# One small copy of the gates' weights, six times on GpSimd instead of ScalarE

## The chip, the cores and the metric

The kernel is one program on one core of a Trainium2 chip. A core has five engines, each with its own stream of instructions: TensorE (PE in the profile; its weight loads are PEld), VectorE (DVE), ScalarE (ACT), GpSimd (POOL) and SyncE (SP), which here only issues transfers. An engine executes its stream strictly in order; an instruction that waits for another engine or a transfer (a DMA) holds back all that stand behind it on its own engine. The metric is the device time of one launch in microseconds.

## The reference

For each of 8 batches `x` (2496 rows of 256 features, float32) is filtered in the frequency domain, and the result goes through a mixture of 8 experts, of which each row uses the two with the highest gate:

```python
X = np.fft.rfft(x, axis=1)
y = np.fft.irfft(X * (filt_r + 1j * filt_i)[None], n=x.shape[1], axis=1)

x = y.reshape(B * S, D)
noisy = x @ w_gate + np.log1p(np.exp(x @ w_noise)) * noise
top2 = np.argpartition(-noisy, 2, axis=1)[:, :2]      # softmax over these two: top2_w
for e in range(E):
    for k in range(2):
        mask = top2[:, k] == e
        h = np.maximum(x[mask] @ w1[e], 0.0)
        out[mask] += top2_w[mask, k, None] * (h @ w2[e])
```

Result: 19968 rows of 256 float32.

## The kernel before, in words

**The filter.** The transforms of a batch are matrix products with constant tables (2496 = 39 x 64). Features are taken in two halves of 128; `n` counts halves of batches, so `n` = 0 and 1 are batch 0, and `n % 2` (`h`) says which half. For each half the steps are: `s1` (L339, and L388 for its evictions), `kg1` (L417, with the filter applied by VectorE in L435 and L436), `kg2` (L457; the eviction into `G` is L459), then `t3` and `i2`. `t3` (L541) transposes `G` on TensorE into a PSUM tile, and ScalarE copies that to the tile `tf` (L546). `i2` (L563) multiplies by the last table, and ScalarE copies the product into the tile `yt` (L575). From `yt` SyncE writes up to 4 x 117 rows of the result to the array `y` in memory (L582). `t3` and `i2` run six times in a half, for 22 groups of rows (five times four groups, once two).

**The gates.** For the second half of a batch `yt` has 8 columns more, and into these goes `dense`, the weight that each expert has for the row; a row of `y` so carries what the experts need later. That is L580, a copy of 117x32 numbers (117x16 the last time), which stands between L575 and L582. `dense` comes from the gating of the batch: logits (L469, L479, L510), an exponential on ScalarE (L824, which first loads an activation table), and a chain of small VectorE operations that ends in L845. In parallel VectorE computes ranks (L835), and TensorE counts with them (L848 to L850) where each row goes in the lists of its experts. `slots` (L931, L932, L958) and `route` (L1000 to L1026; TensorE in L981 and L1017) turn this into the lists of rows, which GpSimd writes to memory with an indirect transfer (L1029, `lst`).

**The tiles.** In `n` = 0 the `yt` tiles lie in three places of other tiles that are not yet in use; for odd `n` they share two buffers (L572, `bufs=2`). So the third `yt` of a second half can be written only when the first has been read by its transfer, and so on.

**The experts.** A list is read back (L1050, `lt`), made into row numbers (L1058), and four indirect gathers fetch 128 rows each from `y` (L1096). GpSimd reorders halves of numbers (L1148) and takes the weights (L1115, `gt`). TensorE transposes the rows (L1156, `xps`), ScalarE and VectorE split them into a high part `mxh` (L1159) and a low part, and then come the two matrix products with each expert's weights: `hps` and `yps` (L126 to L128 in both, L1282 and L1283 for `yps` later on). Expert blocks start while the filter still works on later batches, and the two are interleaved.

**The order.** What stands where on an engine is fixed when the program is built. For the first batches a plan (`fft_stream`, with `at(slot, ...)`) lists the steps by slot and `pin` holds their instructions on each engine in the order in which they were written; the gating and the routing are placed freely between them. A timeline that the builder keeps for all engines decides where such free instructions go, and a different engine for one instruction changes this timeline for what follows. L580 is one of the instructions that `pin` holds in order on its engine.

Of the kernel before, what the change touches and what calls it, by code (L numbers as in the profile page):

```python
# [148 lines left out]
class Moe:  # L149
# [405 lines left out]
    def i2(self, n, g0):  # L555
        nc, P, h = self.nc, self.P, n % 2
        Dh, Dl = self.cD
        th, tl = self.t3t.pop((n, g0))
        k = min(4, NG - g0)
        m = 128 * k  # L560
        p = self.ps("q6")
        if tl is None:
            nc.tensor.matmul(p[:RP, :m], self.rD, th[:120, :m], start=True, stop=True)  # L563
        else:
            nc.tensor.matmul(p[:RP, :m], Dh, th[:120, :m], start=True, stop=False)  # L565
            nc.tensor.matmul(p[:RP, :m], Dh, tl[:120, :m], start=False, stop=False)  # L566
            nc.tensor.matmul(p[:RP, :m], Dl, th[:120, :m], start=False, stop=True)  # L567
        w = 128 + E * h
        if n == 0:
            yt = P.tile([RP, 4, 128], F32, name="yt", tag=("mxl0", "mxh1", "mxl1")[g0 // 4 % 3], bufs=1)  # L570
        elif n == 2:
            yt = P.tile([RP, 4, 128], F32, name="yt", tag="hl", bufs=8)  # L572
        else:
            yt = P.tile([RP, 4, 128 + E], F32, name="yt", bufs=2)
        e = nc.scalar.copy(yt.bitcast(U16)[:, :k, :256].rearrange("p g (two d) -> p g two d", two=2),  # L575
                       p.bitcast(U16)[:RP, :2 * m].rearrange("p (g d two) -> p g two d", g=k, two=2))
        if n == 2:
            self.yev.append(e)
        if h:
            nc.scalar.copy(yt[:, :k, 128:], self.dense[:, g0:g0 + k])  # L580
        y = self.y[BLK + n // 2 * ROWS:BLK + (n // 2 + 1) * ROWS].rearrange("(p g) d -> p g d", p=RP)
        w = nc.sync.dma_start(y[:, g0:g0 + k, h * 128:h * 128 + w], yt.bitcast(I32)[:, :k, :w])  # L582
        if n == 2:
            self.yw2 = w
# [826 lines left out]
```

## Time and profile before

| | |
|---|---|
| median of 3 runs | 2192.69 us (2189.25 to 2193.18) |
| profiled execution, its time | 2190.66 us |
| its span (first to last instruction) | 2189.0 us |
| TensorE busy | 2150.6 us, 98% |
| VectorE busy | 1570.2 us, 72% |
| ScalarE busy | 1164.0 us, 53% |
| GpSimd busy | 974.3 us, 45% |

All positions below are microseconds from the start of the span. The profiled execution is 2.03 us shorter than the median of the runs. The names `q_996`, `q_1003` and so on in the listings of the order are those that the builder gives to PSUM tiles, in the order in which they are made; the trace leaves the numbers out.

### The profile page before, as it was taken

To read this page: it belongs to the slowest core of one execution; us is meant where nothing else is said; L and a number is where in the kernel's file an instruction comes from. 1 tells how busy PE (TensorE), PEld (TensorE's weight loads), DVE (VectorE), ACT (ScalarE), POOL (GpSimd) and SP (SyncE) were. 2 spreads that over 40 slices of the span, in tenths; PEclk is the share of its full clock that TensorE was granted. 3 is DMA by queue.
4 is the path that set the end of the run, shared out by engine and by line. 5 is a ranking of instruction groups with operands and counts; after the bars stand their busy time and mean duration, and the time that the engine had idled before them with its cause. 6 is when DMAs were issued, how large, how long until landed. Compare 5 with 4: busy or idle time off the path is not lost.

```text
span 2189.0 us, 37935 instructions
## 1 busy us (share of the span) xinstructions
PE 2150.6 (98%) x12217; PEld 1809.7 (83%) x12217; DVE 1570.2 (72%) x3388; ACT 1164.0 (53%) x2242; POOL 974.3 (45%) x825
## 2 busy tenths in 40 slices
PE   8899999999999999999999999999999999999998
PEld 6658888888888888888888888888888888888897
DVE  4777788868877977787757976597555555565676
ACT  6565655765566456545645455444444444454565
POOL 4036245345433544354344544455455444454552
PEclk9999999999999999999999999999999999999999
DMA  8778878987987767667665667555565557678984
GB/s 248 226 221 218 209 171 196 207 192 167 211 208 181 150 158 181 152 144 168 149 138 125 154 138 170 107 124 127 112 128 113 121 110 140 155 172 164 219 201 97
DMA packets 443828, 359.55 MB, mean 164 GB/s; under 512 B 201499, under 2 KB 360963, under 8 KB 443619
## 3 DMA queue, kind: packets, MB, share of 16 engines
q1 hardware_dynamic: 382371, 272.89, 48.6%
q0 software_dynamic: 61248, 84.14, 23.2%
q8 instruction: 98, 1.61, 0.3%
q14 instruction: 111, 0.91, 0.2%
HBM read 212.85 MB, written 105.12 MB: 145 GB/s over the span
## 4 chain that ended last, share of the span: by engine, by line
PE 90%; DMA 4%; DVE 2%; ACT 2%; issue 1%; POOL 1%; SPq 0%; POOLq 0%; ACTq 0%; DVEq 0%
PE yps L1282 20%; PE hps L126 13%; PE hps L127 13%; PE hps L128 13%; PE yps L1283 10%; PE yps L126 3%; PE yps L128 3%; PE yps L127 3%; PE q L457 3%; PE q L541 1%; DMA stage<-w 1%; PE q L565 1%; PE u L493 1%; PE q L566 1%; PE q L567 1%
## 5 line engine op out<-in xcount | busy, mean ns | idle before, releaser
L1292 POOL DMA_INDIRECT out<-stage,ids x315 | 535.9, 1701 | 370.6 <-DVE stage L1291 197.2
L1282 PE MATMUL yps<-w,hh 128*128 128x512 f32 x1944 | 682.5, 397 | 2.0 <-ACT hh L1251 1.9
L1096 POOL DMA_INDIRECT stage<-y,ids x315 | 343.3, 1090 | 523.2 <-DMA xt<-stage 411.8
L1283 PE MATMUL yps<-w,hl 128*128 128x256 f32 x1944 | 515.5, 281 | 0.0
L127 PE MATMUL hps<-mxl,w1h 128*128 128x512 f32 (+2 forms) x1312 | 506.5, 387 | 0.0
L1252 DVE SCALAR_TENSOR_TENSOR hl<-hps,hh 128x512 fp32r<-128x512 f32 (+2 forms) x656 | 425.9, 663 | 109.3 <-ACT hh L1251 95.1
L128 PE MATMUL hps<-mxh,w1l 128*128 128x512 f32 (+2 forms) x1312 | 503.3, 385 | 0.0
L126 PE MATMUL hps<-mxh,w1h 128*128 128x512 f32 (+2 forms) x1312 | 493.8, 390 | 2.4 <-DVE hl L1252 1.3
L1251 ACT ACTIVATE hh<-hps 128x512 fp32r<-128x512 f32 (+2 forms) x656 | 370.0, 583 | 206.7 <-PE hps L128 188.9
L1282 PEld LDWEIGHTS yps<-w,hh 128*128 128x128 f32 x1944 | 354.2, 188 | 75.0 <-ACT hh L1251 2.9
L1283 PEld LDWEIGHTS yps<-w,hl 128*128 128x128 f32 x1944 | 364.7, 188 | 26.2 <-DVE hl L1252 0.2
L1289 ACT ACTIVATE stage<-yps,gt 128x256 f32<-128x256 f32 x315 | 142.3, 477 | 386.4 <-PE yps L1283 198.0
L1291 DVE SCALAR_TENSOR_TENSOR stage<-yps,gt,stage 128x256 f32<-128x256 f32 x243 | 112.0, 480 | 255.1 <-ACT stage L1289 215.0
L128 PEld LDWEIGHTS hps<-mxh,w1l 128*128 128x128 f32 x1312 | 247.0, 188 | 50.8 <-issue 0.5
L127 PEld LDWEIGHTS hps<-mxl,w1h 128*128 128x128 f32 x1312 | 246.8, 188 | 42.8 <-issue 1.1
L126 PEld LDWEIGHTS hps<-mxh,w1h 128*128 128x128 f32 x1312 | 243.2, 188 | 45.4 <-DVE hl L1252 5.2
L1206 ACT CAST w1h<-stage 128x512 fp32r<-128x512 f32 x200 | 123.7, 623 | 117.1 <-DMA stage<-w 51.8
L1208 DVE TENSOR_TENSOR w1l<-stage,w1h 128x512 fp32r<-128x512 f32 x204 | 138.3, 684 | 45.7 <-ACT w1h L1206 32.5
L126 PE MATMUL yps<-w,hh 128*128 128x256 f32 x576 | 162.5, 287 | 4.7 <-ACT hh L1251 4.2
L128 PE MATMUL yps<-w,hl 128*128 128x256 f32 x576 | 158.7, 285 | 1.6 <-DVE hl L1252 1.6
L127 PE MATMUL yps<-w,hh 128*128 128x256 f32 x576 | 159.4, 284 | 0.0
L1208 DVE TENSOR_TENSOR w<-stage,w 128x512 fp32r<-128x512 f32 x220 | 146.4, 683 | 5.5 <-ACT w L1206 4.8
(247 smaller groups left out, 2903.7 us busy)
## 6 DMA issues: line engine op xcount, KB each, us to landing
stage<-w SPq DMA_DIRECT2D x424, 256.0 KB
x<-x SPq DMA_DIRECT2D x88, 256.0 KB
fx<-fd SPq DMA_DIRECT2D x140, 128.0 KB
fd<-c SPq DMA_DIRECT2D x73, 240.0 KB
out<-z SPq DMA_DIRECT2D x24, 702.0 KB
y<-yt SPq DMA_DIRECT2D x40, 248.6 KB
y<-yt SPq DMA_DIRECT2D x40, 234.0 KB
wb<-w SPq DMA_DIRECT2D x8, 1024.0 KB
```

What stands on the lines that cost most here:

```text
L126: nc.tensor.matmul(o, lh, rh, start=start, stop=False)
L127: nc.tensor.matmul(o, lh, rl, start=False, stop=False)
L128: return nc.tensor.matmul(o, ll, rh, start=False, stop=stop)
L1096: self.pin(lambda: nc.gpsimd.indirect_dma_start(out=x.bitcast(I32), out_offset=None, in_=self.y[:BLK + ready * ROWS], in_offset=bass.Indir ...
L1206: (cast or nc.scalar.copy)(h, sv)
L1208: nc.vector.tensor_sub(l, sv, f32v(h))
L1251: self.lastr = r = nc.scalar.activation(h, p, AF.Relu)
L1252: v = nc.vector.scalar_tensor_tensor(l, p, 0.0, f32v(h), op0=ALU.max, op1=ALU.subtract)
L1282: nc.tensor.matmul(bank, h, hl, start=(f == 0), stop=False)
L1283: self.mm = nc.tensor.matmul(p, l, hl[:, 0], start=False, stop=(f == 7))
L1289: nc.scalar.activation(o, p, AF.Copy, scale=gate[:, t])
L1292: a = nc.gpsimd.indirect_dma_start(out=self.io["out"][:BLK + ready * ROWS], out_offset=bass.IndirectOffsetOnAxis(ap=ids[:, t:t + 1], axis= ...
```

## The change

In `i2`, for `n` = 1 only, the copy of `dense` into `yt` is issued to GpSimd (`tensor_copy`) and no longer to ScalarE (`copy`). It concerns six copies of the 48 in the program; the other halves keep theirs.

```diff
@@ -577,7 +577,7 @@
         if n == 2:
             self.yev.append(e)
         if h:
-            nc.scalar.copy(yt[:, :k, 128:], self.dense[:, g0:g0 + k])
+            (nc.gpsimd.tensor_copy if n == 1 else nc.scalar.copy)(yt[:, :k, 128:], self.dense[:, g0:g0 + k])
         y = self.y[BLK + n // 2 * ROWS:BLK + (n // 2 + 1) * ROWS].rearrange("(p g) d -> p g d", p=RP)
```

With it the builder places other instructions in another order too, as far as about 800 us into the program; from there to the end the order is the same. Three places follow.

ScalarE at the end of batch 0's second half (`q_946` to `q_1003` are products of `t3` and `i2`, `ge` is the exponential of the gates):

```order
 L546 COPY tf<-q_946 120x512
 L575 COPY yt<-q_953 117x4x256
+L546 COPY tf<-q_959 120x512
+L575 COPY yt<-q_966 117x4x256
 L824 ACT_TABLE_LOAD
 L824 ACTIVATE ge<-gd 117x22
-L580 COPY yt<-dense 117x4x8
-L546 COPY tf<-q_959 120x512
-L575 COPY yt<-q_966 117x4x256
-L580 COPY yt<-dense 117x4x8
 L459 COPY G<-q_980 128x64x8
 L546 COPY tf<-q_996 120x512
```

The eviction `tf` of `q_959` and the `yt` after it stand ahead of the exponential now, and no copy of `dense` stands between them; the four later copies of `dense` in this half are gone from ScalarE as well, and all six stand on GpSimd, one after the other, behind its last addition of the early filter (L442).

TensorE at the same place (`rk` are the three small products that count ranks):

```order
 L457 MATMUL q_980<-cf,ab 128x2x64
 L457 MATMUL q_980<-cm,ab 128x2x64
+L541 MATMUL q_996<-ident,G 120x128 x4
+L563 MATMUL q_1003<-tf,cm 117x512
+L541 MATMUL q_1009<-ident,G 120x128 x4
+L563 MATMUL q_1016<-tf,cm 117x512
+L417 MATMUL q_1023<-fx,cm 128x512
 L848 LDWEIGHTS half
 L848 MATMUL rk<-sum_79,half 128x8
```

Five groups of the filter's products have moved ahead of the counting, and with the counting the later steps of the lists (L931, L958, L981, L1017) stand further back among the filter's work.

ScalarE at the first expert block, in the kernel before (`mxh_1766` and `mxh_1775` are the two halves of the block's rows):

```order
L1159 CAST mxh_1766<-xps 128x512
L546 COPY tf<-q_1452 120x512
L575 COPY yt<-q_1459 117x4x256
L580 COPY yt<-dense 117x4x8
L546 COPY tf<-q_1465 120x512
L575 COPY yt<-q_1472 117x4x256
L1159 CAST mxh_1775<-xps 128x512
```

And in the changed kernel:

```order
L575 COPY yt<-q_1472 117x4x256
L580 COPY yt<-dense 117x4x8
L388 COPY c_1480<-q_1478 120x512
L1159 CAST mxh_1766<-xps 128x512
L388 COPY stage<-q_1483 120x512
L546 COPY tf<-q_1516 120x512
L575 COPY yt<-q_1523 117x4x256
L580 COPY yt<-dense 117x4x8
L546 COPY tf<-q_1529 120x512
L575 COPY yt<-q_1536 117x4x256
L1159 CAST mxh_1775<-xps 128x512
```

Both `mxh` stand further back: the first behind the evictions of `q_1452` to `q_1478`, the second behind those of `q_1516` to `q_1536` also, two of which fill `yt` tiles. TensorE's products of the block stand further back too: its first transpose (L1156) behind `q_1478`, its second and the first `hps` behind `q_1542`.

## Rows read from the trace of the kernel before

**Rows 1.** The page's part 4: the chain that ended last, by engine.

```profile
PE 90%; DMA 4%; DVE 2%; ACT 2%; issue 1%; POOL 1%; SPq 0%; POOLq 0%; ACTq 0%; DVEq 0%
```

**Rows 2.** PE's waits from 60 to 200 us: total us, times, longest us.

```profile
PE q L541 <- ACT tf L546: 4.2, 3, 2.9
PE xps L1156 <- POOL stage L1148: 2.3, 2, 1.5
PE u L469 <- ACT G L459: 0.7, 1, 0.7
PE q L417 <- ACT G L459: 0.2, 1, 0.2
```

**Rows 3.** ACT's timeline: start us, duration us, line, operation, [idle before <-releaser].

```profile
70.97 1.28 ACT L824 ACT_TABLE_LOAD   x1
76.64 0.22 ACT L580 COPY yt<-dense 117x32 f32<-117x32 f32 x1 [4.15 <-DVE dense L845]
76.76 0.58 ACT L546 COPY tf<-q 120x512 f32<-120x512 f32 x1
80.25 1.01 ACT L575 COPY yt<-q 117x1024 uint16<-117x1024 uint16 x1 [0.77 <-PE q L563]
87.47 1.01 ACT L575 COPY yt<-q 117x1024 uint16<-117x1024 uint16 x1 [2.02 <-DMA y<-yt]
```

**Rows 4.** Busy us by stretch: PE, PEld, DVE, ACT, POOL, PE clock, DMA share, GB/s.

```profile
74.00:77.30 3.30, 0.46 (x6) 0.20 (x4) 3.30 (x17) 0.66 (x3) 0.00 (x0) 0.98 0.17 49
77.30:79.00 1.70, 1.60 (x5) 1.23 (x6) 1.63 (x12) 1.67 (x5) 0.00 (x0) 0.50 0.52 148
79.00:81.00 2.00, 2.00 (x7) 1.10 (x6) 1.97 (x16) 1.23 (x2) 0.00 (x0) 0.60 0.70 200
```

**Rows 5.** PE's timeline around the end of batch 0's second half.

```profile
66.30 0.60 PE L541 MATMUL q<-ident,G 128*120 128x128 f32 x4
77.39 1.11 PE L541 MATMUL q<-ident,G 128*120 128x128 f32 x4 [2.92 <-ACT tf L546]
84.38 0.38 PE L541 MATMUL q<-ident,G 128*120 128x128 f32 x2
```

**Rows 6.** All copies of line 580: ns min/median/max, first and last start.

```profile
L580 ACT COPY yt<-dense x48: 203/218/262, 76.6 to 1508.9; 117x32 f32<-117x32 f32 x40, 117x16 f32<-117x16 f32 x8
```

**Rows 7.** All of GpSimd's copies of line 1115, its small copies.

```profile
L1115 POOL COPY gt<-stage x82: 178/786/2225, 132.2 to 2148.2; 128x4 f32 x74, 128x2 f32 x5, 128x3 f32 x3
```

**Rows 8.** The queue of SyncE: the transfers of result rows.

```profile
76.88 1.95 SPq L582 DMA_DIRECT2D y<-yt  x2
137.78 0.33 SPq L582 DMA_DIRECT2D y<-yt  x2
```

**Rows 9.** GpSimd's timeline: the write of the first list, and its read.

```profile
107.93 1.61 POOL L1029 DMA_INDIRECT lst<-ro,row  x1 [59.77 <-DVE ro L1026]
114.16 1.21 POOL L1050 DMA_DIRECT2D lt<-lst  x2
```

**Rows 10.** PE's timeline, from the logits of batch 1 to the first expert block.

```profile
111.02 1.41 PE L469 MATMUL u<-G,wg 128*32 128x360 f32 x16 [0.68 <-ACT G L459]
130.99 0.66 PE L1156 MATMUL xps<-ident,stage 128*128 128x128 f32 x4 [0.77 <-POOL stage L1148]
135.05 0.60 PE L1156 MATMUL xps<-ident,stage 128*128 128x128 f32 x4
136.77 0.50 PE L126 MATMUL hps<-mxh,w1h 128*128 128x512 f32 x1 [0.42 <-PE hps L128]
```

**Rows 11.** ACT's timeline around the first expert block.

```profile
134.61 0.22 ACT L580 COPY yt<-dense 117x32 f32<-117x32 f32 x1 [0.51 <-DVE rank L835]
136.12 0.60 ACT L1159 CAST mxh<-xps 128x512 fp32r<-128x512 f32 x1
143.30 1.01 ACT L575 COPY yt<-q 117x1024 uint16<-117x1024 uint16 x1 [1.32 <-DMA y<-yt]
```

**Rows 12.** PE's timeline: the second list's first block.

```profile
196.80 0.66 PE L1156 MATMUL xps<-ident,stage 128*128 128x128 f32 x4 [1.54 <-POOL stage L1148]
```


## The prediction

> **What bounds the kernel now.** I read the page's chain first: 90% of it is TensorE work [rows 1], so the time changes by what TensorE waits, and by what it does at the lower clock. The second view is TensorE's waits in the stretch that the change reaches first [rows 2]: the longest is 2.92 us, a transpose (L541) that waits for ScalarE's `tf` (L546). The third is ScalarE's timeline there [rows 3]. The first copy of `dense` starts at 76.64 after 4.15 us of idling until VectorE's L845; the `tf` that TensorE needs stands right behind it, at 76.76 to 77.34, though its product had long been there. VectorE is busy for all of 74.00 to 77.30 [rows 4], so `dense` can't come earlier. The fourth view is the table of stretches [rows 4]: after that wait TensorE works at a granted clock of 0.50 (1.2 GHz) up to 79.00 and at 0.60 on the mean of the next 2 us; the same four transposes that took 0.60 us at 66.30 took 1.11 at 77.39 [rows 5]. The half level costs 1.70 x 0.50 + 2.00 x 0.40 = 1.65 us. So this one place is worth 2.92 + 1.65 = 4.57 us, if nothing else held the work back. My claim is that most of it is given back: two `yt` buffers take over the wait, and the expert block that follows is placed worse.
>
> **What it removes and adds.** ScalarE loses six copies of 0.22 us [rows 6], 1.3 us in all; this is worth nothing by itself, since ScalarE idles 4.15 us there. GpSimd gets six copies. It has stood idle for 59.77 us when it comes to L1029 at 107.93 [rows 9], so nothing is queued behind them before the list. No row shows this copy on GpSimd. Its small copies in L1115 take 178 ns at least, 786 at the median and 2225 at most [rows 7]; beneath, ScalarE's 218 ns is the nearest for the same tile. I take 0.25 us, near the minimum, because only these two run there, and keep 0.18 and 2.2 for the range. SyncE's transfer of a `yt` (L582) now waits for GpSimd and not for ScalarE.
>
> The Trainium skill speaks against this ("SBUF — State Buffer", section "Who interferes with whom"): a GpSimd instruction that reads this memory and a VectorE instruction with two inputs in it share a pair of ports, and the second one waits until the first is done. VectorE's chain of small two-input operations is busy throughout [rows 4], so by that rule GpSimd's copies run late and VectorE's steps are held up by them; the wide spread in [rows 7] agrees with it. By that rule the copies take the median or far more, and the sum would be that of rival D.
>
> **The first wait, step by step.** `tf` of `q_959` and its `yt` come before the table load (70.97 to 72.25 [rows 3]), about 1.6 us that ScalarE now spends earlier; the exponential ends at about 74.2, when VectorE first asks for it, and `dense` is ready at about 76.5 as before. TensorE goes from `q_980` on through `q_996` with no wait and at full clock. GpSimd's first copy ends at 76.5 + 0.25 = 76.75, and SyncE issues the transfer at about 76.8, as before at 76.88 [rows 8]. The next `yt` of the ring (`q_1003`) must wait until this transfer has landed. Before, ScalarE wrote that buffer at 80.25 [rows 3], so the round trip was at most 80.25 - 76.88 = 3.37 us; I take 79.7. From there `yt` 1.0 and `tf` 0.58 end at about 81.2, and TensorE's last transpose of the half (`q_1038`) runs then, against 84.38 before [rows 5], after a wait of about 1.9 us. A lead of 3 us; but the fifth `yt` waits for a transfer again, as the one at 87.47 did for 2.02 us [rows 3]. Its transfer is issued behind SyncE's other work, which runs about 1.4 us earlier, so `yt` comes at 86.0 and the products after it have a lead of 1.4 us. Two further waits for `G` that go, 0.68 and 0.24 [rows 2], make it 2.3 at the logits of batch 1 (L469 at 111.02 [rows 10]). **Term 1: -2.3 us**; its bounds are -4.57 (the wait and the half clock both gone) and 0 (each turn of the ring as late as before).
>
> **The first expert block.** The counting (L848 to L850) now stands behind five groups of products, and each later step of the lists behind more of the filter. `ro` (L1026) gets behind VectorE's evictions of the logits (L479), so the list is written at 110.2 in place of 107.93 [rows 9]. From there to the first transpose of the block (130.99 [rows 10]) is a chain of transfers of 130.99 - 107.93 = 23.06 us, which nothing shortens: 133.3. TensorE stands at 130.22 (130.99 less 0.77) - 2.3 = 127.9. The work between the two L1156, 135.05 - 130.99 less about 0.5 for the first one's transposes, so 3.5 us [rows 10], now stands ahead of it and takes it to 131.4: a wait of 1.9. Next, `q_1483` waits for ScalarE, whose L580 of batch 1 waits for VectorE's gates, as at 134.61 [rows 11]: about 0.85. Then the second transpose and three `hps`, until 140.5. The next `hps` needs `mxh_1775`. Before, that cast ran at 136.12 [rows 11]; now it stands behind `yt` of `q_1523` and of `q_1536`. `q_1523` waits for the transfer of a `yt` issued at 137.78 [rows 8], as it did before until 143.30 [rows 11], 5.5 us after the issue. With 143.30 less a little for the earlier filter, then two `yt` of 1.0, a `tf` and the cast, partly overlapping, `mxh_1775` is there at 144.5: a wait of 4.0. In all 1.9 + 0.85 + 4.0 = 6.75 us against 0.77 + 0.42 = 1.19 before [rows 10]. **Term 2: +5.5 us.** If that transfer takes only the 3.37 us of the earlier one, the wait is about 1.3 and the term +2.9; if the transfers of the list are also quicker by the 1.9 us, it is +1. At the upper end it is +8, if the issue slips by another 2.5 us behind the weights' loads.
>
> **The clock again.** A wait of 4 us is longer than the one of 2.92 us after which the clock fell to half. **Term 3: +1.65 us**, bounds 0 and 3.3 (once more after the 1.9 us wait).
>
> **The second list.** In the new order TensorE has 157 instructions between the last step of batch 1's route and the next wait for `xps`, against 138, and the write of the list stands behind two scatters on GpSimd in place of three. The wait of 1.54 us at 196.80 [rows 12] may go. **Term 4: -1.5 us**, bounds -1.5 and 0.
>
> **Sum.** -2.3 + 5.5 + 1.65 - 1.5 = +3.35 us. On the profiled execution, 2190.66, this is 2194.0; that execution lies 2.03 us under the median of the runs, so on the median 2192.69 it is 2196. Until about 800 us the order goes on to differ, with no place where I can price it; I give it +-3 us.
>
> **The rivals.** A time within 0.2% (4.4 us) can't be told from no change here, so 2188.3 to 2197.1 counts as the same.
>
> A, the forecast: 2196, own range 2193 to 2200. For it: the waits for `yt` transfers that the trace already shows [rows 3, 11]; against it: it rests on one cast's place behind two `yt`.
>
> B, the gain stays: the wait and the half clock both go, and the block's later start is hidden by filter work. 2192.69 - 4.57 = 2188.1. For it: this is the largest wait before 200 us [rows 2]. Against it: the buffers and the 23.06 us of transfers.
>
> C, it cancels: the `yt` transfer of `q_1459` takes 3.37 us, the wait for `mxh_1775` is 1.3 and doesn't lower the clock. -2.3 + 2.9 - 1.5 = -0.9, 2191.8. The change then does in effect nothing: the six copies weren't the bound, the transfers are.
>
> D, slower: GpSimd's copies take 2.2 us each, the most in [rows 7], while VectorE is busy [rows 4]. The place is the ring of two `yt`, two turns of which (`q_1003` and the fifth) are on TensorE's path: each 2.2 - 0.25 = 2.0 later, 4.0 in all, and the wait before `q_1038` grows from 1.9 to 3.9 and halves the clock, another 1.65. 3.35 + 5.65 = +9.0, 2201.7. It decides from a copy of about 1.25 us on, where that wait passes 2.92. Against it: 0.18 us also occurs.
>
> **Chances.** A 0.42, C 0.23, B 0.15, D 0.13, and 0.07 for the rest of the order on either side. Faster: of B two thirds, of the rest half, 0.13. Slower: D, a third of A, and the rest's other half, 0.13 + 0.14 + 0.04 = 0.31, with 0.03 more for D's weaker forms inside C: 0.34. Same: 0.53. The range for 8 in 10: from B's upper half, 2189, to D, 2202.
>
> **What would show it.** In the profile after: `tf` ahead of L824 on ScalarE and no wait of 2.92 us at 77; the six copies on GpSimd near 0.25 us (D: over 1.25); ScalarE's `yt` at about 79.7 and 86 waiting for `y<-yt`; L469 at 108.7; the list at 110.2, the first `xps` near 133.3; an `hps` that waits about 4 us for `mxh` near 140 to 145, the clock half after it. It is wrong if that wait is under 1.3 us (C) or absent (B), or if a stretch between 200 and 800 us moves the end by more than these terms.

## The result and the profile after

The changed kernel takes 2208.93 us (median of 5 runs, 2207.32 to 2216.39), the kernel before 2193.18 us in the runs beside it (2189.25 to 2193.81): ratio 1.0088, 95% interval 1.0073 to 1.0103. That is 0.9% slower, and above the forecast range. The profiled execution took 2212.77 us.

The page, its span and TensorE's row of part 1:

```profile
span 2211.0 us, 37919 instructions
...
PE 2160.1 (98%) x12217; PEld 1815.1 (82%) x12217; DVE 1572.6 (71%) x3388; ACT 1166.8 (53%) x2236; POOL 976.3 (44%) x831
```

TensorE is busy 2160.1 - 2150.6 = 9.5 us longer with the same 12217 matmuls, which is the lower clock (added up by the granted clock of each microsecond to 2160 us, work at half clock costs 12.4 us here and 3.3 us before); it is idle 2211.0 - 2160.1 = 50.9 us against 38.4. Together these are the 22 us by which this profiled execution is longer. So both halves count: waits, and what the clock does behind them.

TensorE's longest waits from 60 to 1000 us (total, times, longest), the stretch of [rows 2] and what follows it; two lines of before, then after:

```profile
PE yps L126 <- ACT hh L1251: 4.2, 3, 1.7
...
PE lg L522 <- ACT uh L514: 1.5, 1, 1.5
```

```profile
PE yps L126 <- ACT hh L1251: 6.1, 3, 5.4
PE hps L126 <- ACT mxh L1159: 4.3, 2, 2.6
PE lg L522 <- ACT uh L514: 3.4, 1, 3.4
PE q L541 <- ACT tf L546: 2.9, 3, 1.5
PE q L457 <- ACT G L459: 2.4, 2, 2.1
PE xps L1156 <- POOL stage L1148: 2.0, 1, 2.0
PE rk L848 <- DVE sum L831: 1.9, 1, 1.9
```

The longest wait of before, 2.92 us for `tf`, is gone; what is left under that name is three waits of 1.5 us at most. Elsewhere waits are longer: 5.4 us for `hh` (1.7 before), 3.4 us in the logits (L522; 1.5 before), 2.6 us for `mxh` (0.5 before).

**The end of batch 0's second half.** ScalarE there (start, duration, line, idle before), against [rows 3]:

```profile
71.31 0.61 ACT L546 COPY tf<-q 120x512 f32<-120x512 f32 x1
...
73.15 1.28 ACT L824 ACT_TABLE_LOAD   x1
...
80.13 1.01 ACT L575 COPY yt<-q 117x1024 uint16<-117x1024 uint16 x1 [4.28 <-DMA y<-yt]
...
87.25 1.01 ACT L575 COPY yt<-q 117x1024 uint16<-117x1024 uint16 x1 [3.94 <-DMA y<-yt]
88.69 0.59 ACT L575 COPY yt<-q 117x512 uint16<-117x512 uint16 x1 [0.43 <-POOL yt L580]
```

The eviction `tf` (71.31) is now ahead of the table load (73.15), as the order said. But the third and the fifth `yt` wait 4.28 and 3.94 us for a transfer of result rows, and the sixth 0.43 us for GpSimd's copy. TensorE waits for what stands behind these:

```profile
81.68 0.43 PE L541 MATMUL q<-ident,G 128*120 128x128 f32 x2 [1.47 <-ACT tf L546]
...
83.36 0.69 PE L563 MATMUL q<-tf,cm 120*117 120x256 f32 x2 [0.39 <-ACT tf L546]
...
89.82 0.49 PE L457 MATMUL q<-cf,ab 128*128 128x128 f32 x2 [2.12 <-ACT G L459]
```

```profile
111.49 1.41 PE L469 MATMUL u<-G,wg 128*32 128x360 f32 x16 [0.48 <-ACT G L459]
...
117.88 0.64 PE L522 MATMUL lg<-uh,hl 120*117 120x352 f32 x1 [3.41 <-ACT uh L514]
```

1.47 + 0.39 + 2.12 = 3.98 us have taken the place of 2.92. The logits of batch 1 start at 111.49, before at 111.02 [rows 10]. That lag of 0.47 us is older than the change: the last transposes of batch 0's logits (L510) start at 55.91 in this trace and at 55.42 in that of before. So from there to the logits of batch 1 the change has won and lost nothing: the half clock behind 2.92 us is gone too, and the new waits have cost as much.

**GpSimd's copies** are as short at the median as I had put them; all six, ns min/median/max:

```profile
L580 POOL COPY yt<-dense x6: 198/247/539, 77.0 to 89.3; 117x32 f32<-117x32 f32 x5, 117x16 f32<-117x16 f32 x1
```

**The logits of batch 1.** VectorE ahead of the wait of 3.41 us:

```profile
113.95 2.42 DVE L854 CAST bi<-base 128x8 int32<-128x8 f32 x1
114.39 1.98 DVE L947 TENSOR_SCALAR off<-done 8x1 f32<-8x1 f32 x1
114.45 1.93 DVE L952 TENSOR_SCALAR val<-small 8x32 f16<-8x32 f32 x1
116.43 0.36 DVE L515 TENSOR_TENSOR ul<-u,uh 120x192 fp32r<-120x192 f32 x1
```

and GpSimd beside it:

```profile
113.49 1.61 POOL L1029 DMA_INDIRECT lst<-ro,row  x1 [23.96 <-DVE ro L1026]
114.61 2.79 POOL L1206 CAST w1h<-stage 128x512 fp32r<-128x512 f32 x4
```

Three small operations took 2.42, 1.98 and 1.93 us, all three until 116.4, while GpSimd wrote the list and made its casts; L515, which the logits need, came behind them at 116.43. In the kernel before L854, L947 and L952 take 0.13 to 0.16 us at the median, and at this place 0.23, 0.13 and 0.59, the last beside one of GpSimd's casts. In the last part of that wait and behind it, and behind the one at 362 us, the clock is at half for about seven microseconds (busy times of TensorE, its weight loads, VectorE, ScalarE and GpSimd, then the clock):

```profile
116.00:119.50 3.50, 1.62 (x7) 1.57 (x8) 2.40 (x10) 0.33 (x2) 1.73 (x4) 0.50 0.49 152
119.50:123.00 3.50, 3.50 (x12) 2.25 (x11) 0.25 (x1) 2.94 (x5) 2.10 (x4) 0.53 0.03 1
...
362.00:365.50 3.50, 3.42 (x12) 2.82 (x13) 3.50 (x8) 2.57 (x6) 1.60 (x2) 0.50 1.29 271
365.50:369.00 3.50, 3.50 (x18) 2.46 (x17) 1.08 (x3) 0.23 (x1) 2.51 (x3) 0.56 0.76 259
```

The clock costs only where TensorE works: 1.62 x 0.50 + 3.50 x 0.47 = 2.5 us behind the first wait, 3.42 x 0.50 + 3.50 x 0.44 = 3.3 us behind the second.

**At 362 us** ScalarE waits 8.62 us for weights, with `hh` in its queue behind their cast:

```profile
360.28 1.24 ACT L1206 CAST w1h<-stage 128x512 fp32r<-128x512 f32 x2 [8.62 <-DMA stage<-w]
```

and SyncE, which issues these loads, had other transfers ahead of them:

```profile
344.02 1.27 SPq L396 DMA_DIRECT2D fx<-fd  x2
345.38 0.57 SPq L582 DMA_DIRECT2D y<-yt  x1
346.01 2.11 SPq L307 DMA_DIRECT2D out<-z  x2
348.71 7.14 SPq L1178 DMA_DIRECT2D stage<-w  x4
```

Two loads of the filter (L396), a transfer of result rows, and two transfers of zeros of 702 KB each stand ahead of the first four loads of weights (348.71). SyncE itself waits 7.6 us for VectorE's L408 before it can issue the loads of the filter at 344.02.

### The profile page after: what moved, and what is told of

The parts are those of the page before. It is cut to its first block, busy times and chain, and to the rows that moved or that the text cites. A ratio compares the mean times of both kernels' runs of the same rounds, so it can differ in the third digit from the quotient of the medians.

```text
span 2211.0 us, 37919 instructions
## 1 busy us (share of the span) xinstructions
PE 2160.1 (98%) x12217; PEld 1815.1 (82%) x12217; DVE 1572.6 (71%) x3388; ACT 1166.8 (53%) x2236; POOL 976.3 (44%) x831
## 4 chain that ended last, share of the span: by engine, by line
PE 72%; DVE 1%; issue 0%; DMA 0%; ACT 0%; POOL 0%; POOLq 0%; ACTq 0%; DVEq 0%
PE yps L1282 20%; PE hps L126 11%; PE hps L127 11%; PE hps L128 11%; PE yps L1283 10%; PE q L457 2%; PE q L541 1%; PE yps L126 1%; PE yps L128 1%; PE yps L127 1%; PE q L565 1%; PE q L566 0%; PE q L567 0%; PE u L493 0%; PE q L419 0%; PE q L420 0%
```

## The experiments

They ran in five groups, each on one chip with the kernel before beside it: e1 to e4, e5 to e8, e9 to e12, e13 and e14, e15 to e17. The kernel before takes 2181 to 2188 us there, so ratios to it are compared; the times in the expectations of e1 to e4 were still reckoned for the first chip, with 2193. The changed kernel has 1.0088 on the first chip and 1.0114 on another, with intervals that overlap. Each kernel has a table that lists the instructions of each engine by the names that the builder gives them; the same statement has the same name in both kernels, whatever its engine. The table becomes edges that fix the order of issue and wait for nothing:

```diff
 def tile_kernel(tc, io):
+    block = tc.nc.cur_bb.bb.instructions
     with ExitStack() as ctx:
         Moe(ctx, tc, io).run()
+        in_order(tc, block)    # for each engine: issue_order(table[k], behind=table[k - 1])
```

Where the kernel's own `pin` would contradict the table, its edges are left out. So the order can be kept while the engine of the copies changes, and the other way round; the edits below say which table stands in it.

| | order | copies on | median us | ratio (95%) |
|---|---|---|---|---|
| e12 | before | ScalarE | 2187.94 | 1.0007 (0.9997 to 1.0018) |
| e1 | before | GpSimd | 2185.97 | 1.0015 (1.0005 to 1.0025) |
| e2 | after | ScalarE | 2203.59 | 1.0104 (1.0088 to 1.0121) |
| e8 | after (the changed kernel) | GpSimd | 2206.37 | 1.0114 (1.0088 to 1.0140) |
| e6 | after to 111 us, then before | GpSimd | 2186.91 | 1.0020 (1.0008 to 1.0031) |
| e7 | before to 111 us, then after | GpSimd | 2204.13 | 1.0092 (1.0071 to 1.0114) |
| e9 | before to 171 us, then after | GpSimd | 2203.55 | 1.0076 (1.0063 to 1.0088) |
| e13 | before to 283 us, then after | GpSimd | 2204.19 | 1.0085 (1.0067 to 1.0102) |
| e14 | before to 425 us, then after | GpSimd | 2192.55 | 1.0026 (1.0013 to 1.0038) |
| e15 | after from 283 to 425 us alone | GpSimd | 2195.30 | 1.0059 (1.0044 to 1.0074) |
| e16 | e15, weights first | GpSimd | 2190.88 | 1.0039 (1.0025 to 1.0052) |
| e3 | after, VectorE edit | GpSimd | 2200.30 | 1.0087 (1.0071 to 1.0102) |
| e4 | after, zeros later | GpSimd | 2201.76 | 1.0095 (1.0080 to 1.0110) |
| e11 | after, e3 and e4 | GpSimd | 2199.84 | 1.0066 (1.0053 to 1.0079) |
| e17 | after, e3 and e16 | GpSimd | 2194.76 | 1.0048 (1.0035 to 1.0062) |
| e5 | before, four `yt` buffers | GpSimd | 2183.85 | 1.0004 (0.9992 to 1.0016) |
| e10 | e5, first block later | GpSimd | 2190.28 | 1.0020 (1.0010 to 1.0031) |

e12 is the kernel before against itself; 0.1% can't be told from nothing here. All versions but e12 and e2 have the copies on GpSimd, so each ratio is to be held against e1's 1.0015 too.

### Is it the copies, or the order? (e1, e2, e12, e8)

e1 is the changed kernel with the table of the kernel before:

```diff
-ORDER: none (the builder's own)
+ORDER: kernel before; POOL: L580 x6 behind L442, ACT: without them
```

> The six copies on GpSimd, and on every engine the order of the kernel before, held by a table (TensorE, VectorE and SyncE unchanged; on ScalarE only the six copies are gone; on GpSimd they stand where the changed kernel has them). Theory 1, the loss comes from the changed order of the other instructions: no loss here, 2188 to 2194 us, the wait of 2.92 us and the half clock at 77 us gone or reduced, the logits of batch 1 at 108 to 111 us, and no wait over 2 us before the matmul of L522. Theory 2, the copies on GpSimd themselves hold VectorE or the result rows back: 2200 us or more, with GpSimd's L580 over 1 us or VectorE's operations beside them longer than in the kernel before.

e2 is the kernel before (no change in `i2`) with the changed kernel's table:

```diff
+ORDER: changed kernel; POOL: without L580
+ORDER: ACT: ... L546 tf<-q_996, L580, L580, L575 yt<-q_1003, L580, ...
```

> The order of the changed kernel on every engine, held by a table, but the six copies on ScalarE again, each put just ahead of the first instruction that can't start without it (the first two behind the tf of q_996). Theory 1 (the order): as slow as the changed kernel, 2204 to 2212 us. Theory 2 (the engine of the copies): back to 2190 to 2196 us.

> The kernel before as it is, for a profile on the chip of these runs. Its median is 2181 to 2183 us here, its waits those of its first profile (2.92 us at 77 us, 1.5 us at 115 and 197 us, 1.7 us at 514 us) to within 0.5 us; a ratio of 1.000 within 0.001.

> The changed kernel as it is, on the chip of these runs, to compare with. By every theory a ratio to the kernel before of 1.007 to 1.011, the same waits as in its first profile to within 1 us each, though 362 us may differ, since e2 with the same order waited 3.7 and not 5.4 us there.

The order makes the loss: e2, with the copies on ScalarE, loses 1.04%, and e8 1.14%; e1, with the copies on GpSimd, loses 0.15%, not clearly more than e12's 0.07%.

e12's waits were those of its first profile, but for 0.8 and not 1.7 us for `hh`; its median lies above the 2181 to 2183 us expected, as does that of the kernel before beside it, 2185.32. e8's ratio is just over the 1.011 expected, and its waits are not all those of the first profile to within 1 us: the one at L522 is 3.4 us again, but that for `hh` is 2.1 and not 5.4, that for `G` before L457 0.3 and not 2.1, that for the counting 0.6 and not 1.9, and L339 waits 2.2 and not 0.6. Of these only the wait at L522 came back as it was.

e1 also took the wait at 77 us away and got nothing for it. Its logits start at 113.91 and not at 108 to 111; 1.18 us of this stands in its trace at L510 already (56.67, in e12 55.49), and the rest puts them 1.5 us behind e12's 111.20. ScalarE's wait for the ring, and TensorE's behind it:

```profile
81.08 1.01 ACT L575 COPY yt<-q 117x1024 uint16<-117x1024 uint16 x1 [4.18 <-DMA y<-yt]
```

```profile
90.53 1.68 PE L417 MATMUL q<-fx,cm 128*128 128x512 f32 x2 [1.54 <-ACT G L459]
```

The sixth of GpSimd's copies took 1.30 us in e1, beside VectorE's two-input operations L1000 to L1002, and 0.99 to 1.54 us in the six other traces that keep this order there with two `yt` buffers; the first five took 0.35 us at most in e1. TensorE's wait at 90.53 doesn't come from it: ScalarE began that `G` at 89.89, and the copy starts at 90.05.

### Where does the gain of the removed wait go? (e5, e10)

```diff
-            yt = P.tile([RP, 4, 128 + E], F32, name="yt", bufs=2)
+            yt = P.tile([RP, 4, 128 + E], F32, name="yt", bufs=4)
```

> As e1_order_before (copies on GpSimd, order of the kernel before), but second halves have four yt buffers in place of two, in all batches. In e1 ScalarE waited 4.18 and 4.08 us before a yt (81.08, 88.35), and TensorE 1.54 us for G behind it with 3.4 us of half clock. Theory A, the ring of two gives the gain back: both waits of ScalarE go, the wait for G and the half clock behind it too, and the time is 3 us or more under e1, a ratio to the kernel before of 0.998 to 1.000. Theory B, the lead is lost anyway where the lists are gathered (first xps): the waits near 81 and 88 go but the ratio stays at 1.0015.

With four buffers ScalarE no longer waits there, and the logits start at 109.28, in e12 at 111.20 (0.24 us of this stands at L510 already). The lead is lost at the first rows of the first block, which don't come sooner:

```profile
132.14 1.12 PE L1156 MATMUL xps<-ident,stage 128*128 128x128 f32 x4 [4.22 <-POOL stage L1148]
```

On GpSimd the read of the list (L1050, at 114.40 here, before at 114.16 [rows 9]) stands behind casts of weights that wait for their loads, so this chain doesn't start sooner when TensorE is ahead. That speaks for theory B; the ratio of 1.0004 lies between the two theories' and doesn't differ from e1's beyond the intervals.

e10 puts TensorE's products of the filter into that wait:

```diff
 ORDER of e5, PE:
-L1156 (xps 1), L848 to L850, q_1452 to q_1472, q_1478, L1156 (xps 2), L126
+L848 to L850, q_1452 to q_1472, q_1478, L1156 (xps 1), L1156 (xps 2), L126
```

> As e5_ring4, with one place of the order changed: TensorE's counting of batch 1 (L848 to L850), the products q_1452 to q_1472 and q_1478 stand ahead of the first transposes of the first expert block (L1156) and not between the two, ScalarE's two mxh behind the evictions of q_1452 to q_1472, VectorE's mxl behind dense. In e5 TensorE waited 4.22 us for the first rows of the block, with 6.8 us of half clock behind that. Theory A, that wait is what ate the gain: it falls below 1.5 us, the half clock goes, and the time is 4 to 7 us under e5, a ratio to the kernel before of 0.997 to 0.999. Theory B, the wait only moves to the mxh or to the weights of the next expert: a ratio of 1.000 or more.

Theory B held in the main: the wait of 4.22 us went, others came, though not those it named (1.5 us for the counting and 1.9 us for `mxl`), and the ratio is 1.0020. No version here is faster than the kernel before.

### Which part of the order? (e6, e7, e9, e13, e14)

The tables are spliced: what the first order has placed up to a TensorE instruction, then all else in the second order.

```diff
+ORDER (e6): changed kernel up to the L469 of batch 1's logits at 111 us, then kernel before
+ORDER (e7): kernel before up to there, then changed kernel
+ORDER (e9): as e7, up to L1017 of batch 1; e13, e14: up to TensorE's work at 283, 425 us
```

> Copies on GpSimd; the order of the changed kernel for all that its builder placed ahead of the logits of batch 1 (L469 at 111 us), and from there the order of the kernel before. Theory A, the loss is already laid down by then (the route of batch 0 behind five groups of products, its list late): ratio to the kernel before 1.006 or more, with the long waits at 117 and 135 us. Theory B, the loss comes from the order behind it (first expert block, second list, transfers of zeros ahead of weights): ratio 1.003 or less.

> The mirror of e6: copies on GpSimd; the order of the kernel before up to the logits of batch 1, and from there the order of the changed kernel. Theory A (laid down in the first 111 us): ratio 1.003 or less. Theory B (the order behind it): 1.006 or more, with the waits near 190, 205 and 362 us.

> Copies on GpSimd; the order of the kernel before up to the last step of batch 1's route (L1017, at 171 us), and from there the order of the changed kernel. e7 changed over at the logits of batch 1 (111 us) and lost 0.92%, e6 the other way round 0.2%. Theory A, the loss is that of the first expert block (111 to 171 us) and runs on from there: ratio 1.003 or less. Theory B, most of it comes from the places behind it (L419 and xps at 187 to 205 us, hh at 362, mxh at 565): ratio 1.005 to 1.009.

> As e9, with the change-over from the order of the kernel before to that of the changed kernel at 283 us (in the time of the kernel before) and not at 171. e9 lost 0.76%. Theory A, the loss behind 171 us is spread evenly over the stretches whose order differs, up to 800 us: a ratio to the kernel before of 1.005 to 1.007. Theory B, it is that of 171 to 283 us (the second list's first block, L419 at 187 and 228 us, L493 at 270): 1.003 or less. Theory C, it is that of few places, hh at 353 us and mxh at 564 us: 1.006 to 1.008.

> As e13, with the change-over at 425 us, behind the stall of hh at 353 us. Theory A (evenly): 1.003 to 1.004. Theory C (few places): that of mxh at 564 us alone is left, 2 to 4 us, 1.001 to 1.002.

e6 and e7 rule out theory A: the first 111 us, in which the copies stand, carry about 0.2% (0.3% at the interval's end), hardly more than e1's 0.15%, and what comes behind carries 0.9%. By e9 theory B held. e13's 1.0085 lies above the numbers of all three theories, and its interval takes in C's; e14's 1.0026 is between the theories' numbers. By e7, e9 and e13 the stretch from 111 to 283 us adds little that these intervals can show; from e13 to e14, on one chip, the loss falls from 0.85% to 0.26%. So some 0.6%, 13 us of 2185, lies in 283 to 425 us. Of the 0.26% that is left the copies alone make 0.15% (e1), so that the order behind 425 us costs anything is not shown. In the traces e13 and e14 differ from e1 in order, engine by engine, from 333 and 482 us on, both up to 726 us and not 800: the stretch that the two splices part is in fact 333 to 482 us.

### What in that stretch? (e15, e16)

> Copies on GpSimd; the order of the kernel before, but that of the changed kernel in the stretch from 283 to 425 us alone. e13 (changed from 283 us on) lost 0.85%, e14 (from 425 us on) 0.26%. Theory A, the stretch costs by itself what their difference says: a ratio to the kernel before of 1.004 to 1.007, and a long wait for hh near 350 us with half clock. Theory B, a loss shows only where what follows is changed too: 1.002 or less.

```diff
 ORDER of e15, SP, at 340 us:
-L396, L396, L582, L307, L307, L1178 x4, L1127 x3, L1178 x2, L1127, L1178 x2
+L1178 x4, L396, L396, L582, L1127 x3, L1178 x2, L1127, L1178 x2, L307, L307
```

> As e15, but on SyncE in that stretch the first four loads of the next expert's weights (L1178) stand ahead of two loads of the filter (L396) and a transfer of result rows (L582), and the two transfers of zeros (L307) behind all eight loads. In e13 the first of these loads was issued at 339.5 us behind L396, which SyncE could not issue before 336.2; in the kernel before (e12) it was issued at 332.8. Theory A, this order on SyncE is the cause: the wait for hh falls below 1.5 us and the ratio to 1.000 to 1.002. Theory B, the weights' buffers come free late or the transfers are slow: the wait stays above 3 us and the ratio at that of e15.

e15 alone costs 0.59%; without the 0.15% of the copies (e1) that is 0.44%, which agrees with the difference of e13 and e14 within the intervals. SyncE in the kernel before (e12), in e15, and in e16:

```profile
332.77 6.51 SPq L1178 DMA_DIRECT2D stage<-w  x5
...
347.31 1.12 SPq L307 DMA_DIRECT2D out<-z  x2
```

```profile
337.46 1.27 SPq L396 DMA_DIRECT2D fx<-fd  x2
338.83 0.56 SPq L582 DMA_DIRECT2D y<-yt  x1
339.43 1.36 SPq L307 DMA_DIRECT2D out<-z  x2
341.00 6.91 SPq L1178 DMA_DIRECT2D stage<-w  x4
```

```profile
331.76 11.95 SPq L1178 DMA_DIRECT2D stage<-w  x4
343.76 1.27 SPq L396 DMA_DIRECT2D fx<-fd  x2
```

The weights are issued from 332.77 in e12, from 341.00 in e15 behind a load that could not go before 337.46, from 331.76 in e16. SyncE's wait for that load in e15:

```profile
SPq L396 <- DVE oc L1000: 12.8, 1, 12.8
```

TensorE's waits in e15 from 283 to 425 us, and in e16:

```profile
PE yps L126 <- ACT hh L1251: 5.1, 1, 5.1
PE ra L981 <- DVE oc L1001: 2.0, 2, 1.8
```

```profile
PE ra L981 <- DVE oc L1001: 2.0, 2, 1.8
```

The wait of 5.1 us for `hh` is gone in e16: shown to come from SyncE's order. The median falls from 2195.30 to 2190.88 (one of e16's eight runs is above the fastest of e15's six), and the ratio to 1.0039, which is neither theory's number. So this order on SyncE is worth about 0.2%, 4.4 us, a little under half of the 0.44%. What keeps the rest, 0.24% above e1 (the wait for `ra`, with half clock behind it in e16, or what follows), was not settled.

### The two stalls in the changed kernel (e3, e4, e11, e17)

```diff
 ORDER of the changed kernel, DVE (e3):
-L854, L947, L952, L515, L855, L856, L515, L857, L515
+L515, L515, L515, L854, L947, L952, L855, L856, L857
 SP (e4): L307 x2 behind the eight L1178; e11: both; e17: e3, and SP as in e16
```

> The order of the changed kernel, but on VectorE the six small operations of the next list's base (L854, L947, L952, L855 to L857) stand behind the three L515 of batch 1's logits, not ahead of them and between them. In the changed kernel three of them took 2.42, 1.98 and 1.93 us at 114 us beside GpSimd's list write and casts, and the matmul L522 waited 3.41 us, with 6.8 us of half clock after it. Theory A, only these operations are held up by GpSimd, and they hold up L515: the wait falls to about 1.4 us, the half clock goes, 5 us less than the changed kernel, 2202 to 2205 us. Theory B, L515 itself is held up by GpSimd just as they are: the wait stays at 3 us or more and the time at 2208 to 2210.

> The order of the changed kernel, but on SyncE two transfers of zeros (L307, 702 KB each, issued at 346 us) stand behind the weights' loads (L1178) of the next expert and not ahead of them. In the changed kernel ScalarE waited 8.62 us for these weights and TensorE 5.36 us behind it, at 362 us. Theory A, the zeros delay the weights: the wait falls below 1.5 us and the half clock after it goes, 6 to 8 us less, 2200 to 2203 us. Theory B, the weights are late because their buffers come free late: the wait stays above 3 us and the time at 2207 to 2210.

> The changed kernel's order with the edits of e3 (small VectorE operations behind L515) and e4 (zeros behind the weights) together. Theory A, the stalls are separate and their costs add: about 8 us under the changed kernel on this chip (2206), 2196 to 2200 us. Theory B, what one place gives back is lost at the next: 2201 us or more, as each alone.

> The changed kernel's order everywhere, with e3's edit on VectorE and e16's on SyncE. Both stalls gone, what is left is the rest of the changed order: a ratio to the kernel before of 1.002 to 1.005 (e11, with the zeros alone moved, had 1.0066). If the two places are not the main part, 1.006 or more.

e3: VectorE with the list write now from 113.28 to 114.89 and GpSimd's casts from 114.39 on, and TensorE's matmul of the logits:

```profile
113.74 0.36 DVE L515 TENSOR_TENSOR ul<-u,uh 120x192 fp32r<-120x192 f32 x1
...
115.24 0.90 DVE L854 CAST bi<-base 128x8 int32<-128x8 f32 x1
```

```profile
115.08 0.43 PE L522 MATMUL lg<-uh,hl 120*117 120x352 f32 x1 [0.83 <-ACT uh L514]
```

L515 ran in 0.36 us beside the list write, during which L854 had stood still in the changed kernel, and its two others in 0.22 and 0.26 us beside the casts; L854, behind them, still took 0.90 us. The wait for L522 is 0.83 us and no half clock follows. The Trainium skill ("SBUF — State Buffer", section "Who interferes with whom") has this: casts and `tensor_scalar` can take the ports that VectorE shares with GpSimd, when their operands meet certain conditions, and outside such modes an operation with at most one input in that memory, as L515 with its other one in PSUM, doesn't meet GpSimd there. The rows agree with it for these operations.

The ratios: e3 1.0087 and e4 1.0095 are each lower than e8's 1.0114, within the intervals (in e4 the longest wait for `hh` is 1.2 us); e11 1.0066 and e17 1.0048 are clearly lower than that, e17 also than the 1.0088 of the first chip. So the two stalls, mended together, give back about half of the loss. In e4 the weights are issued no sooner (348.68), but their first cast waits 0.94 and not 8.62 us: without the zeros ahead of them they land in time, and theory A held for the wait. That the time fell so little is not explained; e4 has waits that the first profile has not, 2.3 us for `G` before L493 and 2.2 us before L339, and e8 has them too (1.8 and 2.2).

## Why the prediction was wrong

**Right.** The sign: slower, which the prediction gave 0.34 and "same" 0.53. The wait of 2.92 us went, the copies took 0.25 us at the median, the ring of two `yt` took the wait over: ScalarE's third `yt` came at 80.13 (forecast 79.7). Rival D, slow copies in the ring, is out: 198 to 539 ns here, and the slow sixth copy of e1 has no third `yt` waiting for it in this half.

**Term 1 (-2.3 us).** The mechanism was right and the size off: the logits start 0.47 us later than before, which is the lag from ahead of the change, and not 2.3 earlier. The term is 0, its own bound. The fifth `yt` came at 87.25, not 86.0, the sixth had to wait for GpSimd's copy, and `G` behind it cost TensorE 2.12 us, which the sum didn't have (in e8 that wait is 0.3 us, and the logits gain 0.2 us since L510). The two waits for `G` that were to go stayed, at 0.24 and 0.48 us.

**No term for the logits.** The prediction let VectorE's L479 and the list's last step change places and priced only the list. The list is written at 113.49 and not 110.2, which brought GpSimd's list write and casts beside VectorE's small operations; that cost 3.4 - 1.5 = 1.9 us of waiting (1.5 is the wait at L522 in the trace of before) and 2.5 us of half clock. The prediction weighed such contention at L580, where the copies took 0.54 us at most in this trace; it bore on this place 37 us later.

**Terms 2 and 3 (+5.5 and +1.65 us).** Waits did come there, but in part others: TensorE waits 1.88 us for the counting (L848), whose VectorE chain ran late from the logits and lost more at its end (L818 and L827 took 0.97 and 1.17 us, 0.33 at the median, beside GpSimd's copies L1148 at 132.12), not for `xps`, and 1.7 us for `mxh`, not 4.0. The way to that `mxh` was as forecast, behind a `yt` that waits 2.02 us for a transfer (146.33).

```profile
135.61 0.17 PE L848 MATMUL rk<-sum,half 128*128 128x8 f16 x1 [1.88 <-DVE sum L831]
...
149.54 0.50 PE L126 MATMUL hps<-mxh,w1h 128*128 128x512 f32 x1 [1.71 <-ACT mxh L1159]
```

The clock fell behind both (busy times, then the clock):

```profile
136.00:140.00 4.00, 4.00 (x12) 2.06 (x11) 3.90 (x29) 2.30 (x4) 2.89 (x4) 0.57 0.94 250
150.00:154.00 4.00, 3.90 (x11) 1.74 (x11) 0.67 (x5) 0.99 (x3) 0.13 (x1) 0.57 0.54 142
```

With 0.58 us before L339 at 142.04 the waits make 4.2 us against 1.19, +3.0, and the half clock 4.00 x 0.43 + 3.90 x 0.43 = 3.4 us. The sum, 6.4, is near the forecast 7.15, but by luck: the waits grew by less than the forecast 5.5 us, and the clock fell twice and not once. That it falls behind a wait longer than 2.92 us was the prediction's reason for term 3; here it fell behind 1.88 and 1.71 us, and after the 2.12 us at 89.82 it stayed at 1.00.

**Term 4 (-1.5 us).** Wrong: the wait for `xps` of the second list is 2.0 us (1.54 before), not gone, and 1.65 us of half clock stands behind it.

**The step that failed** is the last of the sum: "Until about 800 us the order goes on to differ, with no place where I can price it; I give it +-3 us." That remainder is most of the loss: e9 loses 0.76% (17 us) with nothing changed before 171 us but the copies, which make 0.15% by themselves (e1), so the order behind 171 us costs some 13 us; e15 loses 0.59% in one stretch alone. A part of it could have been found: the order shows that at 340 us SyncE's four loads of weights had gone behind two loads of the filter, a transfer that waits and 1.4 MB of zeros, and e16 prices this place at about 4.4 us. The prediction did name a stretch between 200 and 800 us as a sign of being wrong, but gave the rest of the order 0.07, half of it to either side, and no rival stood for it.

**Open.** Why e16 still loses 0.39%, 0.24% more than e1; why e4's mended wait gave back so little; whether the order behind 425 us costs anything (e14 0.26%, e1 0.15%, intervals that overlap); and e1's 0.15%, which these runs can't separate from no change.

## What to carry to other kernels

When a builder places instructions by its own timeline, a change of one small instruction is a change of the order on every engine: price the order, queue by queue, before the instruction. Look first at the queue that issues the loads: a load that has moved behind a transfer that waits shows up much later, as an engine that waits for its cast. A wait taken from an engine that others keep in step is worth only what the next dependency allows: here the ring of two tiles, then the gathers of the first block.

## What the runs showed of the hardware that was not expected

A 128x8 cast on VectorE that takes 0.15 us took 2.42 us beside GpSimd's list write and casts, and an operation with one operand in PSUM (L515) was not held up beside the same list write (0.36 us). The cost of a wait on TensorE is not its length alone: behind waits of 3.41 and 5.36 us its work at half clock (1.2 GHz) cost 2.5 and 3.3 us more, and behind waits of 1.88 and 1.71 us 1.7 us each.
